# Two-layer kernel behind linear attention: where the second layer's weights and inputs are split into hi and lo, and in which order its first product runs

## The chip, the cores and the metric

The kernel runs on one core of a Trainium2 chip. The metric is device time in microseconds of one execution, as the median of the runs shown. TensorE (PE), VectorE (DVE), ScalarE (ACT), GpSimd (POOL) and SyncE (SP) run side by side; SP issues most transfers, POOL some.

## The reference

```python
q_s = softmax(q, axis=-1); k_s = softmax(k, axis=2)        # with 1e-9 in the divisor
kv  = einsum('bhsd,bhse->bhde', k_s, v)
x   = einsum('bhsd,bhde->bhse', q_s, kv)                   # 8 x 8 heads x 576 x 64
x   = x.transpose(0, 2, 1, 3).reshape(4608, 512)
x   = (relu(x @ w_in1) ** 2) @ w_out1                      # layer 1: 512 -> 2048 -> 512
h   = x @ w_in2
out = (h * (1 / (1 + exp(-h)))) @ w_out2                   # layer 2: 512 -> 2048 -> 512
```

All is float32. The kernel multiplies float32 in three passes of a narrower format: each operand is split into hi (the rounded value) and lo (the rest), and wh·xh + wh·xl + wl·xh is summed.

## The kernel before

**Tiling.** The 4608 tokens are nine blocks of 512 (NB = 9). The hidden width of 2048 is 16 slices of 128 (NF), or eight chunks of 256 (NG).

**First layer.** For each block, 16 steps ("slots") run: `layer_in(f)` is 12 matmuls of 512 columns for one slice, `hidden` makes Relu on ACT, the square (on DVE, but on ACT in the first and last block), and a copy to hi on ACT; `hidden_lo` subtracts on DVE; `layer_out` adds the slice into four PSUM banks two slots later. Beside it stand the next block's attention (`side`, by slot) and the preparation of the second layer's weights: `round_to_dram` loads one of 32 pieces of raw weights, rounds it (one ACT and three DVE operations for each half; phase 3's pieces also an ACT copy that permutes columns) and writes it to `wd` in DRAM from POOL. It is a generator: it goes on by two steps a slot. After a block's last slice `layer_out` copies the four banks into `x2_tile`, makes four sums and writes the seven slots for that block to `x2d` from SP.

**Second layer.** It multiplies by a seven-product scheme on halves of 256: `PRODUCTS` lists which slot of the input (A11, S3, S2, S1, A12, A22, S4) goes with which weight (B11, T3, T2, T1, B21, N4, B22). Blocks go in pairs (`supers`): four pairs, 512 columns wide, and the last block alone, 256 wide. Phase 2 computes h for all of them in the order 0, 1, 2, 4 (the narrow one), 3; phase 3 computes out in the order 0 to 4. A step is one product of one chunk: six matmuls. In phase 2 the chunk j is the outer loop and the product n the inner one; in phase 3 the product is outer and the chunk inner.

`seven(ph, x)` makes one chunk's weight set in SBUF: four loads of 128 KB from `wd` on SP, four subtracts on POOL, then for each of the seven a copy to hi on ACT and a subtract to lo on DVE. It runs in the last block (for phase 2) and in the last pair of phase 2 (for phase 3). `factor(u, n)` loads the two halves of one input slot from `x2d` and `a_split` splits them on ACT and DVE; a pair's factors stay for all eight chunks and are replaced, one by one, in the last chunk of the pair before. Phase 3's inputs come through `stream`: loaded 14 steps ahead (`a_load`), split 6 steps ahead (`a_split`).

`after` evicts a product: ACT copies it or makes Silu, DVE adds it to earlier ones in an output tile `st` (two such tiles; `g_tile` and `x2_tile` have the same two places before). After the seventh product POOL writes two slots to `g2d`, one sum is made on POOL and three on DVE, and POOL writes the rest.

**What orders the work.** 89 tiles of 256 KB ("rooms") are handed out and taken back in a queue by `room` and `back`; a load starts when the room's last reader is done. Eight PSUM banks go round in the same way. From the last block of the first layer on every engine keeps program order (`keep_in_program_order`); before that the framework orders the instructions of each engine by its own plan. All engine calls pass through `InOrder.call` (line 73), so the trace has L73 for all and is read by tile names: `al` and `ah` are lo and hi of an input, `wB`, `wT`, `wN` the weight sets, `a` to `e` PSUM banks of the products, `h` and `acc` those of the first layer.

## Time and profile before

| | us |
|---|---|
| runs (three) | 1642.99, 1646.23, 1646.77; median 1646.23 |
| the profiled execution | 1643.94 |
| its span | 1642.2 |
| PE busy | 1575.8 (96%) |
| DVE busy | 1121.7 (68%) |
| ACT busy | 738.1 (45%) |
| POOL busy | 288.0 (18%) |
| mean granted clock of PE | 0.989 |

The span goes from the first instruction's start to the last one's end. A busy share counts instructions that run; matmuls overlap one another, so PE's busy time is longer than what its columns need, and idle time on PE is what stands between them. A wait is put down to the engine and tile that ended it. A granted clock of 1.00 is 2.4 GHz, 0.5 is 1.2 GHz.

### The profile page before, as it was taken

What the parts mean: (1) busy time and instruction counts of PE and PEld (TensorE: products, weight loads), DVE (VectorE), ACT (ScalarE), POOL (GpSimd) and SP (SyncE); (2) the same over time, 40 slices, a digit from 0 to 9 for tenths busy, and PEclk for the clock granted to TensorE, in tenths of its full rate; (3) what the DMA queues carried; (4) which work ended last, traced back from release to release, by engine and by line L of the source; (5) the groups of instructions that cost most, each with busy time, mean ns of one, the idle gap of its engine ahead of it and who ended that gap; (6) DMA issues with size and microseconds to landing.
All of it is one profiled execution on the core that took longest, in us unless ns stands there. A gap on an engine that the chain in (4) does not pass through costs nothing. (4 is left out here: it accounts for less than half of the span.)

```text
span 1642.2 us, 23717 instructions
## 1 busy us (share of the span) xinstructions
PE 1575.8 (96%) x7672; PEld 1293.0 (79%) x7672; DVE 1121.7 (68%) x2284; ACT 738.1 (45%) x1562; POOL 288.0 (18%) x517
## 2 busy tenths in 40 slices
PE   5999999999999999999999999998998799999998
PEld 3767888877878888888888778787976688888888
DVE  8999676676757677672356776767778856656565
ACT  7875343333434344342365343333344644444433
POOL 2000101000101010000022534444756300000000
PEclk9999999999999999999999999999999899999999
DMA  9635343343524434230233565655667668676845
GB/s 261 194 111 158 113 149 113 101 145 92 158 85 132 129 109 143 86 122 0 76 111 105 196 243 205 244 194 216 234 216 278 236 194 246 195 243 179 260 127 166
DMA packets 225787, 269.49 MB, mean 164 GB/s; under 512 B 61568, under 2 KB 159616, under 8 KB 225664
## 3 DMA queue, kind: packets, MB, share of 16 engines
q1 hardware_dynamic: 202416, 193.01, 39.5%
q0 software_dynamic: 21888, 74.46, 12.1%
q8 instruction: 60, 0.98, 0.2%
q10 hardware_dynamic: 1360, 0.52, 0.1%
q14 instruction: 63, 0.52, 0.1%
HBM read 160.17 MB, written 107.74 MB: 163 GB/s over the span
## 5 line engine op out<-in xcount | busy, mean ns | idle before, releaser
L73 PE MATMUL h<-x,wh 128*128 128x512 f32 x1152 | 359.7, 392 | 5.2 <-ACT wh L73 3.3
L73 PE MATMUL acc<-st,wh 128*128 128x512 f32 x1152 | 361.2, 393 | 0.3 <-DVE st L73 0.3
L73 PEld LDWEIGHTS h<-x,wh 128*128 128x128 f32 x1152 | 215.4, 188 | 55.6 <-ACT wh L73 6.6
L73 ACT CAST ah<-al 128x512 fp32r<-128x512 f32 (+1 forms) x350 | 195.4, 578 | 140.5 <-PE d L73 39.6
L73 PEld LDWEIGHTS acc<-st,wh 128*128 128x128 f32 x1152 | 213.2, 188 | 45.7 <-DVE st L73 1.5
L73 DVE TENSOR_TENSOR al<-al,ah 128x512 fp32r<-128x512 f32 (+1 forms) x350 | 206.0, 644 | 50.2 <-ACT ah L73 47.1
L73 PE MATMUL h<-x,wl 128*128 128x512 f32 x576 | 225.3, 391 | 0.2 <-DVE wl L73 0.2
L73 PE MATMUL acc<-st,wl 128*128 128x512 f32 x576 | 224.4, 390 | 0.0
L73 PE MATMUL a<-ah,wB 128*128 128x512 f32 (+1 forms) x640 | 199.8, 375 | 8.6 <-DVE wB L73 6.8
L73 ACT ACTIVATE st<-st 128x512 f32<-128x512 f32 (+1 forms) x120 | 70.7, 589 | 230.7 <-DVE st L73 180.2
L73 ACT ACTIVATE g<-h 128x512 f32<-128x512 f32 x144 | 85.6, 594 | 172.5 <-PE h L73 172.1
L73 DVE TENSOR_TENSOR st<-g,st 128x512 fp32r<-128x512 f32 x144 | 100.0, 695 | 80.5 <-ACT st L73 72.9
L73 PEld LDWEIGHTS a<-ah,wB 128*128 128x128 f32 x640 | 119.9, 193 | 31.3 <-DVE wB L73 8.4
L73 DVE TENSOR_TENSOR st<-st 128x512 f32<-128x512 f32 (+1 forms) x156 | 131.5, 848 | 6.7 <-ACT ah L73 0.5
L73 DVE TENSOR_TENSOR g<-g 128x512 f32<-128x512 f32 x112 | 76.8, 685 | 85.8 <-ACT g L73 85.7
L73 POOL DMA_DIRECT2D g2d<-st x200 | 111.5, 562 | 116.9 <-ACT st L73 87.8
L73 PEld LDWEIGHTS h<-x,wl 128*128 128x128 f32 x576 | 108.3, 188 | 24.0 <-DVE wl L73 1.7
L73 PEld LDWEIGHTS acc<-st,wl 128*128 128x128 f32 x576 | 108.1, 188 | 23.2
L73 ACT CAST st<-g 128x512 fp32r<-128x512 f32 x144 | 89.4, 621 | 74.3 <-DVE g L73 73.2
L73 PE MATMUL a<-al,wB 128*128 128x512 f32 (+1 forms) x320 | 119.7, 374 | 0.2 <-DVE al L73 0.2
L73 PE MATMUL d<-ah,wB 128*128 128x512 f32 (+1 forms) x320 | 100.4, 377 | 10.8 <-DVE st L73 8.6
L73 PE MATMUL b<-ah,wT 128*128 128x512 f32 (+1 forms) x320 | 98.9, 372 | 3.4 <-ACT ah L73 3.4
(131 smaller groups left out, 2496.9 us busy)
## 6 DMA issues: line engine op xcount, KB each, us to landing
al<-g2d SPq DMA_DIRECT2D x224, 256.0 KB, 3.2
g2d<-st POOLq DMA_DIRECT2D x64, 512.0 KB, 3.0
g2d<-st POOLq DMA_DIRECT2D x112, 256.0 KB, 3.6
wraw<-in_moe_w_in_dram SPq DMA_DIRECT2D x64, 256.0 KB, 3.2
wraw<-in_moe_w_out_dram SPq DMA_DIRECT2D x64, 256.0 KB, 3.3
x2d<-st SPq DMA_DIRECT2D x18, 896.0 KB, 6.0
al<-x2d SPq DMA_DIRECT2D x56, 256.0 KB, 3.9
v<-in_v_dram SPq DMA_DIRECT2D x64, 128.0 KB, 2.8
```

What stands on the lines that cost most here:

```text
L73: got = fn(*a, **kw)
```

## The change

- `seven` is no longer run in the second layer. It runs in blocks 1 to 7 of the first layer, two or three sets a block (`SETS`): it loads the raw rows of a chunk, rounds them (phase 3's permutation is now part of the last DVE add, in two pieces), makes the four differences on DVE, splits all seven, and writes each product's hi and lo (256 KB) to `wd` from POOL. Its scratch is the seven rows of `x2_tile`. `round_to_dram` is gone.
- `w_load` loads one product's weights of one chunk, hi and lo, into a room: 56 loads for each phase, for phase 2 in the last block, for phase 3 in the last pair as rooms come free, product by product.
- `layer_out` hands the end of a block to a generator, `keep_outputs`: copies, sums, then for each of seven slots a copy to hi on ACT, a subtract in place on DVE, and two writes to `x2d` from POOL. It goes on during the next block's first slots; for the last block during phase 2's first steps.
- `factor` is four loads (hi and lo of both halves) and no split.
- Phase 2 takes the chunks in pairs: for each product first chunk j, then j + 1, with two sets of PSUM banks and both `st` tiles in use.
- All squares of the first layer are on ACT, all sums of `after` on DVE.

```diff
-    def round_to_dram(ph, f):
...
+    def seven(ph, x, places):
+        lo_, hi_ = slice(0, HB), slice(HB, TB)
+        r0, r1, u0, u1, t, *ws = places
+        raw = [raw_load(ph, x), raw_load(ph, NG + x, (r0, r1))]
         for _ in range(3):
             yield
+        for r, u in zip(raw, (u0, u1)):
+            yield from rounding(ph, r, u, t)
...
+        ws = (*ws, r0, r1)
+        ve.tensor_tensor(t3, b22, b12, op=ALU.subtract)
+        ve.tensor_tensor(b12, b12, b11, op=ALU.subtract)
         yield
+        ve.tensor_tensor(t2, b22, b12, op=ALU.subtract)
+        yield
+        all_ = dict(B21=b21, B11=b11, T3=t3, T2=t2, T1=b12, N4=b21, B22=b22)
+        for m, (name, v) in enumerate(all_.items()):
+            w = ws[m % 4]
+            hi, lo = w[:, lo_], w[:, hi_]
+            ac.copy(hi.bitcast(F32R), v)
+            ve.tensor_tensor(lo, v, hi, op=ALU.subtract)
+            if m == 0:
+                ve.tensor_tensor(b21, b21, t2, op=ALU.subtract)
+            gp.dma_start(out=wd[ph, x][:, names.index(name)], in_=w)
             yield
+    def w_load(ph, x, n):
+        w = W[ph, x, n] = room(F32R, "w")
+        sp.dma_start(out=f32(w), in_=wd[ph, x][:, n])
...
     def hidden(i, n, h):
-        if i in (0, NB - 1):
-            ac.activation(g, g, AF.Square)
-        else:
-            ve.tensor_tensor(g, g, g, op=ALU.mult)
+        ac.activation(g, g, AF.Square)
...
+    def keep_outputs(i):
...
+        yield
         sums(lambda s: t[:, :, s], ve)
+        yield
         u, b = divmod(i, 2)
-        for e in range(2):
-            sp.dma_start(out=x2d[u][e][:, :, b * HB:(b + 1) * HB], in_=t[:, e])
+        for s, _ in PRODUCTS:
+            r = room(F32R, "x2h")
+            hi = r.rearrange("p (e c) -> p e c", e=2)
+            ac.copy(hi, t[:, :, s])
+            ve.tensor_tensor(t[:, :, s], t[:, :, s], f32(hi), op=ALU.subtract)
+            for j, x in enumerate((f32(hi), t[:, :, s])):
+                gp.dma_start(out=x2d[u][:, :, s, j, b * HB:(b + 1) * HB], in_=x)
+            back(r)
+            yield
...
+            for js in ([range(j, j + 2) for j in range(0, NG, 2)] if ph == 2 else [range(NG)]):
+                for n in range(7):
+                    for j in js:
+                        steps.append((ph, u, n, j, u == us[-1]))
...
+        if ph == 2:
+            hi = room(F32R, "ah")
+            for j, t in enumerate((hi, lo)):
+                sp.dma_start(out=f32(t)[:, o], in_=x2d[u][:, c, slot, j])
...
-                sums(at_, ve, gp)
+                sums(at_, ve)
...
+    def load_todo(spare):
+        while todo and len(rooms) >= todo[0][0] + spare:
+            todo.pop(0)[1]()
...
+    SETS = [0, 2, 2, 2, 2, 2, 3, 3, 0]
+            s = SETS[i]
+            for m in range(s + 1):
+                if not doing and made < len(w2list) and s and 3 <= f < NF - 2 and made < sum(SETS[:i + 1]):
+                    doing.append(seven(*w2list[made], [x2_tile[:, x] for x in range(7)]))
+                    made += 1
+                go_on()
...
+            todo += [(1, lambda x=x, m=m: w_load(3, x, m)) for m in range(7) for x in range(NG)]
```

## Rows read from the trace of the kernel before

**Rows 1.** The page, part 1: busy us, share of span, instructions.

```profile
PE 1575.8 (96%) x7672; PEld 1293.0 (79%) x7672; DVE 1121.7 (68%) x2284; ACT 738.1 (45%) x1562; POOL 288.0 (18%) x517
```

**Rows 2.** Stretches: length, busy us of each engine, granted clock, DMA share, GB/s.

```profile
0.00:36.50 36.50, 19.80 (x122) 11.83 (x122) 28.72 (x101) 25.09 (x88) 6.69 (x23) 1.00 0.96 273
36.50:888.90 852.40, 842.93 (x4190) 687.86 (x4191) 581.22 (x1353) 389.72 (x848) 78.62 (x218) 1.00 0.38 115
888.90:1277.50 388.60, 362.75 (x1681) 298.22 (x1680) 284.85 (x439) 154.74 (x320) 191.20 (x263) 0.97 0.63 226
1277.50:1299.57 22.07, 15.26 (x50) 11.25 (x49) 19.14 (x27) 10.42 (x25) 11.52 (x14) 0.81 0.59 209
```

**Rows 3.** Timeline of PE: start us, us; first matmuls of phases 2 and 3.

```profile
888.93 0.39 PE L73 MATMUL a<-ah,wB 128*128 128x512 f32 x1
...
1277.53 0.63 PE L73 MATMUL a<-ah,wB 128*128 128x512 f32 x1
```

**Rows 4.** Chain that ended last, in order of time: start us, us, what.

```profile
1332.74 10.88 PE a L73 x48
...
1617.53 5.76 PE a L73 x48
```

**Rows 5.** Stretches, one for each pair of blocks of phase 2; columns as before.

```profile
888.90:969.00 80.10, 77.75 (x333) 62.98 (x332) 58.19 (x89) 31.42 (x66) 33.96 (x46) 0.98 0.57 208
969.00:1052.00 83.00, 79.85 (x337) 64.67 (x336) 58.71 (x79) 30.69 (x54) 35.39 (x48) 0.96 0.60 220
1052.00:1136.40 84.40, 80.73 (x343) 64.96 (x342) 59.99 (x81) 31.49 (x57) 35.98 (x49) 0.98 0.59 221
1136.40:1184.20 47.80, 43.39 (x337) 42.14 (x336) 34.36 (x75) 18.43 (x53) 31.89 (x47) 0.96 0.60 202
1184.20:1277.50 93.30, 81.04 (x338) 63.47 (x337) 73.60 (x117) 42.71 (x94) 53.99 (x73) 0.98 0.74 263
```

**Rows 6.** Waits of PE from 888.9 to 1299.6: us, times, longest.

```profile
PE d L73 <- DVE st L73: 8.6, 5, 4.7
PE a L73 <- DVE wB L73: 6.8, 2, 4.7
PE b L73 <- DVE al L73: 6.7, 4, 2.0
```

**Rows 7.** Stretches of 4 us at the change to the second pair of blocks.

```profile
968.00:972.00 4.00, 3.97 (x17) 2.78 (x15) 2.35 (x4) 3.05 (x6) 0.54 (x1) 1.00 1.03 399
972.00:976.00 4.00, 1.98 (x7) 1.05 (x6) 3.86 (x6) 2.56 (x6) 1.83 (x2) 1.00 1.02 400
976.00:980.00 4.00, 2.90 (x7) 2.32 (x8) 4.00 (x8) 2.73 (x6) 2.01 (x4) 0.53 0.77 291
```

**Rows 8.** Groups of instructions by form: count, busy us, mean ns, idle before.

```profile
L73 DVE TENSOR_TENSOR al<-al,ah 128x512 fp32r<-128x512 f32 x280 | 180.8, 701 | 38.9 <-ACT ah L73 36.6 <-DMA al<-x2d 1.3 <-DMA al<-g2d 0.7
L73 ACT CAST ah<-al 128x512 fp32r<-128x512 f32 x280 | 169.2, 621 | 121.8 <-PE d L73 33.9 <-PE a L73 22.8 <-PE e L73 20.6
L73 POOL DMA_DIRECT2D g2d<-st x200 | 111.5, 562 | 116.9 <-ACT st L73 87.8 <-ACT wB L73 18.6 <-ACT wT L73 6.8
L73 DVE TENSOR_TENSOR g<-g 128x512 f32<-128x512 f32 x112 | 76.8, 685 | 85.8 <-ACT g L73 85.7
L73 POOL TENSOR_TENSOR st<-st 128x512 f32<-128x512 f32 x32 | 56.6, 1768 | 80.1 <-DVE st L73 44.7 <-ACT st L73 35.5
L73 DVE TENSOR_TENSOR wB<-wB 128x256 fp32r<-128x256 f32 x48 | 22.7, 488 | 8.6 <-ACT wB L73 5.3 <-issue 3.2
L73 ACT ACTIVATE g<-g 128x512 f32<-128x512 f32 x32 | 20.2, 630 | 0.6
```

**Rows 9.** Timeline of DVE: four sums alone, three beside POOL's one.

```profile
889.92 2.75 DVE L73 TENSOR_TENSOR st<-st 128x512 f32<-128x512 f32 x4
...
987.42 3.10 DVE L73 TENSOR_TENSOR st<-st 128x512 f32<-128x512 f32 x3
```

**Rows 10.** DMA issues: KB each, median us from issue to landing.

```profile
wd<-wu POOLq DMA_DIRECT2D x16, 256.0 KB, 3.3
```

More of the change, by code (lines that the diff above doesn't have):

```diff
@@ L142 @@
     x2d = [
-        [dpool.tile([P, 7, len(bl) * HB], F32, name=f"x2d{u}_{e}") for e in range(2)]
-        for u, bl in enumerate(supers)
+        dpool.tile([P, 2, 7, 2, len(bl) * HB], F32, name=f"x2d{u}") for u, bl in enumerate(supers)
     ]
@@ L149 @@
     ]
-    wd = {(ph, f): dpool.tile([P, DM], F32, name=f"wd{ph}_{f}") for ph in (2, 3) for f in range(NF)}
+    wd = {(ph, x): dpool.tile([P, 7, TB], F32, name=f"wd{ph}_{x}") for ph in (2, 3) for x in range(NG)}
     A21, A11, A22, A12, S1, S2, S4 = range(7)
@@ L196, in rounding @@
             )
-            ve.tensor_tensor(o, o, lw, op=ALU.add)
-            back(t)
-            yield
-        if ph == 3:
-            v = room(F32, "wp")
-            ac.copy(
-                v.rearrange("p (e a i) -> p a e i", e=P // Q, a=P // Q),
-                u.rearrange("p (a e i) -> p a e i", e=P // Q, a=P // Q),
-            )
-            back(u)
-            u = v
-        to.append(u)
-    def rounded(ph, raw):
-        to = []
-        for _ in rounding(ph, raw, to):
-            pass
-        return to[0]
+            if ph == 3:
+                to = u.bitcast(I32).rearrange("p (e a i) -> p a e i", e=P // Q, a=P // Q)
+                o, lw = (x.rearrange("p (a e i) -> p a e i", a=2, i=Q) for x in (o, lw))
+                for a in range(2):
+                    ve.tensor_tensor(to[:, 2 * h + a], o[:, a], lw[:, a], op=ALU.add)
+            else:
+                ve.tensor_tensor(o, o, lw, op=ALU.add)
+            if id(t) in lent:
+                back(t)
+            yield
     wh1, wl1, raw1 = {}, {}, {}
@@ L223, in w1_round @@
     def w1_round(x):
-        raw1[x] = rounded(x[0], raw1[x])
+        u = room(F32, "wu")
+        for _ in rounding(x[0], raw1[x], u):
+            pass
+        raw1[x] = u
     def w1_split(x):
@@ L719, in a_load @@
         slot = PRODUCTS[n][0]
-        w = width(u)
-        src = (x2d if ph == 2 else g2d)[u][c]
-        sp.dma_start(out=f32(lo)[:, 0:w], in_=src[:, slot])
-        xs[ph, u, n, c] = [None, lo]
+        o = slice(0, width(u))
+        if ph == 2:
+            hi = room(F32R, "ah")
+            for j, t in enumerate((hi, lo)):
+                sp.dma_start(out=f32(t)[:, o], in_=x2d[u][:, c, slot, j])
+        else:
+            hi = None
+            sp.dma_start(out=f32(lo)[:, o], in_=g2d[u][c][:, slot])
+        xs[ph, u, n, c] = [hi, lo]
     def a_split(ph, u, n, c):
@@ L953 @@
             if n == (NB - 1) * NF:
-                assert nw == len(w2list) and not doing
+                assert made == len(w2list) and not doing
                 back(*kv_rooms[1:])
-                todo = [(9, lambda g=g: seven(2, g, gp)) for g in range(NG)]
-                todo[4:4] = [(4, lambda m=m: factor(LAST_LONG[0], m)) for m in range(7)]
+                todo += [(1, lambda x=x, m=m: w_load(2, x, m)) for x in range(NG) for m in range(7)]
+                todo[28:28] = [(4, lambda m=m: factor(LAST_LONG[0], m)) for m in range(7)]
             if n == NF:
@@ L976 @@
             hidden_lo(n)
-            if not ends:
-                for _ in range(2):
-                    go_on()
-                if i > 0 and nw < len(w2list) and not doing:
-                    doing.append(round_to_dram(*w2list[nw]))
-                    next(doing[-1])
-                    nw += 1
+            s = SETS[i]
[4 more added lines that the diff above has]
+                go_on()
+            if f == NF - 1:
+                assert not doing
+            if ends:
+                load_todo(3)
         else:
@@ L987 @@
                 back(wh1.pop((1, f)), wl1.pop((1, f)))
-                for _ in range(3):
-                    while todo and len(doing) < 3 and len(rooms) - owed[0] >= todo[0][0]:
-                        begin()
-                    go_on()
+                load_todo(3)
     back(*x_rooms, *g_rooms)
```

127 lines of the change are left out of this document (32 added, 95 removed).

## The prediction

> **What bounds the kernel now.** I read the page's busy shares first, then one table of stretches, then TensorE's waits, then what stands around those waits. TensorE (PE) is busy for 96% of the span [rows 1], so only time in which PE stands still or runs at half clock can be won. The table of stretches [rows 2] says where that is: the first layer, 852.4 us long, has 9.5 us of idle PE, and the second layer's first product (phase 2) has 25.9 us in 388.6 us. The first product of phase 3 takes 22.1 us and has 6.8 us idle. How long they could be comes from the chain that ended last: 48 matmuls of 512 columns take 10.88 us and 48 of 256 columns 5.76 us when nothing interrupts them [rows 4], that is 0.2267 and 0.120 us each. Phase 2 has 336 matmuls for each of the five pairs of blocks, four of them wide and one (the last block alone) narrow: 4 x 336 x 0.2267 + 336 x 0.120 = 304.6 + 40.3 = 345.0 us. Its first matmul starts at 888.93 and phase 3's at 1277.53 [rows 3]: 388.6 us, **43.6 us too many**. Phase 3's first product, 48 matmuls, should take 10.9 us and takes 22.0: **11.1 us too many**. Together 54.7 us; the change works nowhere else on the path, so this is nearly all that it can win.
>
> Pair by pair the excess is 3.9, 6.8, 8.2, 7.5 and 17.1 us, each length less 76.2, the short one less 40.3 [rows 5]. The waits name the causes [rows 6]: PE waits for DVE's evictions (8.6 us), for weight sets still being split (6.8) and for factors still being split (6.7). Some of the stops are followed by a granted clock near 0.5, the 1.2 GHz level: 0.53 just after a stretch in which PE was busy 1.98 of 4 us [rows 7]. The first pair's 0.98 over 80.1 us [rows 5] is one such dip and 1.6 us of lost clock; I count 1.7 us for a dip.
>
> **Part by part. Taken out of phase 2:** the 70 splits of factors, each a copy on ACT and a subtract on DVE (0.62 and 0.70 us wide [rows 8]); the splits of the weight sets on both; POOL's subtracts and its share of the sums. One of POOL's adds takes 1.77 us [rows 8], and while it runs DVE's three other sums take 3.1 us; four sums on DVE with POOL quiet take 2.75 us [rows 9]. So the move of the fourth sum onto DVE costs nothing: it even gives back 0.35 us a chunk. What was waited for in [rows 6] is then gone: weights and factors arrive by DMA ready to be multiplied. Next late in their place can only be the DMA itself, which I cost below.
>
> **The pairs of chunks.** A product of one chunk takes 1.36 us, of two 2.72, so a pair takes 19.04 us. DVE's work on it is 10 adds and 8 sums at about 0.69 us: 12.4 us, it fits. PSUM: at most six of eight banks are open at once. The two output tiles (st) are now wanted again sooner: the last product of a first chunk ends 17.7 us into its pair, then add, Silu, sums, and its last write lands about 3.3 us after POOL issues it, as the weights' writes do [rows 10], some 25.3 us into the pair; the next pair writes that tile from about 26.7 us on. DVE waits 0 to 1 us there, and PE would feel it only when DVE is some 5 us late. I take nothing.
>
> **Moved into the first layer.** By the rows' durations [rows 8], DVE loses 112 squares (76.7 us) and gains 16 x 11 half-width operations at 0.49 (86 us) and 56 wide splits at 0.70 (39 us): from 581 to some 630 of 852 us [rows 2]. ACT gains 112 squares at 0.63 (71 us), 112 half-width copies (35 to 70 us, as half or all of a wide one) and 56 wide ones (35 us): from 390 to about 550. POOL issues 80 weight writes and 112 factor writes more at 0.56: about 108 us, beside 79 now. No engine is near its limit, and PE runs two layer-in products ahead of each layer-out. What may hurt is order: seven() works in x2_tile, which keep_outputs() uses too. The load of its second raw rows waits on SP until POOL's last write from that place has landed (3.3 us after its issue [rows 10], plus copy, subtract and issue: some 6 us), and queued behind it are the loads of q, k and v and the round trip of the transposed queries, for which ACT and then PE wait. A slot is about 6 us, so most of it is covered. Bounds: below, a gain of 1 us (SP loses the writes of x2); above, 16 sets x 1 us. I take **3 us**.
>
> **Start of phase 2.** Block 8's seven products are split beside the first products and written by 14 POOL issues, at 0.56 us each. The second output tile is x2_tile's place; those writes, the first some 2 us into phase 2, have landed by about 13 us. PE first feels that DVE waits for it at the seventh product, 16.3 us in, less 1.4 us of DVE work. Covered by some 2 us; I take **1 us** instead of 3.9.
>
> **The transfers.** This is the open term. Factors now take 28 loads of 256 KB between pairs of blocks (7.34 MB) where 14 did, and each weight set of 1.83 MB is read where 0.5 MB was. The room of factor m comes free in the last pair of chunks, and it is wanted one pair later: from 2.7 us into that pair to 35.4 us, 32.7 us for 7.34 MB plus some 5.9 MB of g2d writes (1.83 MB a chunk): 13.2 MB. What can the DMA engines move? In the fullest stretches 399 and 400 GB/s at a share of 1.02 to 1.03 [rows 7]; with small packets 273 at 0.96, or 284 when full [rows 2]. The transfers here are those of rows 7, so I take 390. Then 13.2 MB take 33.9 us: **1.1 us** late at each of two wide changes, and 0.5 us at the narrow one. From the narrow to the last wide pair the window is 25 us for 10.3 MB, 26.4 us: **1.4 us**. In the last pair of blocks the 56 sets for phase 3 are read as rooms come free, ahead of phase 3's first inputs on the same queue. From the first factor load to the eighth input: 7.3 MB of factors, 14.9 MB of sets and inputs, 17.7 MB of writes, 40 MB or 102.5 us, against 91.9 us of matmuls: 10.6 late, less the 1.4 already counted and about 1.5 of writes that can follow: 7.7 us, with a clock dip of 1.7: **9.4 us**.
>
> The Trainium skill (DMA: Bandwidth & Descriptors, section Bandwidth) speaks against that: it has transfers between HBM and SBUF bound at about 358 GB/s for a core. By that figure the residue would be 38.5 us and the time 1628, rival B. The stretches at 399 and 400 GB/s disagree with it; the page itself gives more to a core that streams alone.
>
> **Sum.** Residue: 3 + 1 + 1.1 + 1.1 + 0.5 + 1.4 + 9.4 = 17.5 us. The profiled execution took 1643.94 us, 1.74 us around its span of 1642.2 and 2.3 below the median of the three runs. 1643.94 - 54.7 + 17.5 = 1606.7, said as **1607 us**. About 0.3% (5 us) is what can be told from no change here.
>
> **Rivals.**
> *A. Transfers hide wholly* (phase 3's inputs in time): the residue is 3 to 9 us, 1592 to 1598. For it: the full stretches touch 400. Against: 40 MB in 92 us would want 435.
> *B. The DMA ceiling is lower under reads and writes mixed over 90 us.* A quarter of the way from 390 to 284, at some 360 GB/s, the same sums give 1 + 11.4 (both wide changes, with dips) + 1 + 5.3 + 15.8 + 3 = 37.5: 1627. At 340, about half the way, the residue is 49: 1638. For it: no pair of blocks averages above 263 GB/s [rows 5]. Against: there nothing asked for more.
> *C. Slower, by the same mechanism in the last wide pair and at the start of phase 3:* below about 332 GB/s the residue passes 54.7 us and the kernel loses; at the 284 of the first 36 us it would be 90 us, 1679. Against it: those are small packets, phase 2 moves 2 KB runs.
> *D. The first layer stalls:* SP's wait for x2_tile outlasts its cover. It decides when each of the 16 sets costs PE over 2.3 us, as 16 x 2.3 eats the 37 us; half of that gives 1625. For it: SP carries all loads of attention. Against: PE hardly waits there now.
> *E. POOL's issues slow down beside DVE.* If each took the 1.77 us of POOL's add, the 14 at the start of phase 2 would end 17 us later and PE would stop about 15.5 us, with a dip: 1624. The Trainium skill (SBUF — State Buffer, "SBUF: two separate sides") warns of it: a POOL-issued DMA waits for its descriptors while DVE holds the shared ports. The 200 issues at 562 ns beside a busy DVE do not show it [rows 8].
> *F. The change does not do what it says:* sets arrive too late for the first pair, so the first pair of blocks keeps its 3.9 us and a dip; 1611. The rooms freed in the last block allow all loads by then.
>
> **How the numbers follow.** Forecast (1600 to 1616) 0.50, A 0.15, B 0.18, C 0.03, D 0.09, E 0.02, F 0.03. To leave out no more than 2 in 10 the range goes from 1594 (most of A) to 1632 (B down to about 350 GB/s, the milder half of D). Slower by over 0.3%: C and the worst of D, 0.05; within 0.3%: the edge of B and D, 0.05; faster 0.90.
>
> **What would show it.** Right: phase 2 takes about 350 us from its first matmul to phase 3's, PE's waits for al and wB are gone, DVE has no al subtract there; phase 3's first product stays visibly above 10.9 us with ACT or PE waiting for a DMA from g2d; stretches near 390 GB/s in the last wide pair. Wrong: if that first product takes 11 us (A), if long waits stand at each change of blocks (B), or if 36.5 to 889 has grown by over 10 us (D). I would be wrong altogether if the evictions of two chunks at once held PE in every pair.

## The result, and the profile after

The changed kernel took **1666.55 us** (median of 4 runs, 1664.14 to 1670.69) against 1644.61 for the kernel before on the same chip: ratio **1.0146**, 95% interval 1.0128 to 1.0164 (the two medians alone give 1.0133, inside it). It is slower by about 22 us where 1607 was forecast. The profiled execution took 1670.69 us, 26.8 more than the one of before.

First the table of stretches: length, busy us of each engine with its instructions, granted clock, DMA share, GB/s. The bounds are the first matmuls of phase 2 (917.65) and phase 3 (1306.85) and the end of phase 3's first product.

```profile
36.50:917.65 881.15, 858.62 (x4205) 697.29 (x4203) 584.67 (x1462) 495.81 (x1071) 175.90 (x382) 0.99 0.52 166
917.65:1306.85 389.20, 359.04 (x1681) 299.65 (x1680) 214.97 (x363) 105.53 (x208) 115.03 (x205) 0.96 0.77 284
1306.85:1323.00 16.15, 13.05 (x50) 9.63 (x49) 13.10 (x22) 8.20 (x15) 4.82 (x9) 0.89 1.05 397
```

Against [rows 2, 3]: the first layer's end has moved from 888.93 to 917.65, **28.7 us lost**; phase 2 lasts 389.2 instead of 388.6, **nothing won**; from phase 3's first matmul to the last one it is 354.2 instead of 357.0, 2.8 won. The sum is 26.5 of the 26.8. So there are two questions: what costs the first layer 28.7 us, and where phase 2's expected gain went. In neither is it idle time alone: in the first layer PE stands idle for 22.5 us instead of 9.5, and is busy for 858.6 instead of 842.9 us, as its clock falls behind the stops; in phase 2, 30.2 of the 44.2 us above the 345.0 worked out from [rows 4] are idle. The waits name a place for each (us, times, longest):

```profile
DVE st L74 <- DMA g2d<-st: 111.2, 32, 6.8
PE d L74 <- DVE st L74: 24.2, 12, 3.6
PE xps L74 <- DVE kvs L74: 13.5, 5, 4.6
```

In phase 2, PE's waits for al and wB in [rows 6] are gone, as forecast (3.0 us for al stay in phase 3's first product). In their place DVE waits 32 times for the store of an output tile (st) to land, which it never did before, and PE waits for DVE behind that. In the first layer PE now stops once in each of five blocks for the state of the attention (kvs).

**Phase 2, pair of blocks by pair of blocks** (columns as above; the bounds are the first matmul of each):

```profile
917.65:1002.28 84.63, 78.66 (x338) 63.97 (x337) 50.13 (x78) 27.00 (x48) 26.28 (x45) 0.98 0.71 258
1002.28:1084.08 81.80, 78.37 (x337) 64.06 (x336) 46.56 (x73) 21.80 (x40) 21.40 (x40) 0.98 0.72 271
1084.08:1161.57 77.49, 76.77 (x337) 62.91 (x336) 44.97 (x71) 21.04 (x39) 21.43 (x40) 1.00 0.68 252
1161.57:1219.17 57.60, 44.38 (x338) 43.08 (x336) 30.02 (x74) 14.03 (x42) 23.90 (x40) 0.89 0.70 250
1219.17:1306.85 87.68, 80.86 (x337) 65.63 (x337) 43.29 (x71) 21.66 (x40) 22.02 (x40) 0.95 0.99 373
```

Less 76.2 and, for the narrow one, 40.3, the excess is 8.4, 5.6, 1.3, **17.3** and 11.5 us. The largest single piece lies in the narrow pair of blocks, which was 7.5 before [rows 5].

**Phase 2, the last pair of chunks of the first pair of blocks.** Here the factors of the second pair of blocks are loaded. The timelines of DVE, POOL and PE show the chain (start us, us, instruction, in brackets the idle time before it and its releaser):

```profile
989.19 0.69 DVE L74 TENSOR_TENSOR st<-c,u 128x512 f32<-128x512 f32 x1 [2.57 <-DMA g2d<-st]
989.80 0.68 DVE L74 TENSOR_TENSOR u<-b,u 128x512 f32<-128x512 f32 x1
996.49 0.69 DVE L74 TENSOR_TENSOR st<-c,u 128x512 f32<-128x512 f32 x1 [6.01 <-DMA g2d<-st]
```

```profile
983.94 2.14 POOL L74 DMA_DIRECT2D g2d<-st  x4 [0.66 <-DVE st L74]
```

```profile
997.83 0.50 PE L74 MATMUL d<-ah,w 128*128 128x512 f32 x1 [2.49 <-DVE st L74]
```

DVE stands 2.57 us for the first chunk's tile and 6.01 us for the second's, both because the stores of the pair of chunks before have not landed: the last of them were issued by 986.1 and DVE goes on at 996.5. Its later adds come late and PE stops. Meanwhile the transfer engines are full, which the stretches of 4 us show:

```profile
984.00:988.00 4.00, 4.00 (x20) 3.30 (x19) 1.13 (x2) 0.00 (x0) 2.08 (x4) 1.00 1.02 396
988.00:992.00 4.00, 4.00 (x19) 3.31 (x18) 1.29 (x2) 0.00 (x0) 0.00 (x0) 1.00 1.03 390
992.00:996.00 4.00, 3.34 (x15) 2.44 (x13) 0.00 (x0) 0.00 (x0) 0.00 (x0) 1.00 1.04 397
996.00:1000.00 4.00, 2.17 (x7) 1.75 (x8) 3.08 (x5) 2.14 (x5) 0.13 (x1) 0.83 1.05 400
```

The stores share those engines with the loads of factors. The list of DMA issues (KB each, median us to landing) has them at 5.2 and 6.2 us; before they landed in 3.0 and 3.6, and I had assumed 3.3 [rows 10].

```profile
g2d<-st POOLq DMA_DIRECT2D x64, 512.0 KB, 5.2
g2d<-st POOLq DMA_DIRECT2D x112, 256.0 KB, 6.2
```

**The first layer, the block at 286 us.** `kv_norm` makes kvs from kvps, the product of keys and values, and begins with a reciprocal of one column (rc). Timelines of PE and of DVE:

```profile
275.02 0.29 PE L74 MATMUL kvps<-v 128*64 128x65 f32 x4
...
285.94 0.66 PE L74 MATMUL xps<-qh,st 128*128 128x384 f32 x1 [4.57 <-DVE kvs L74]
```

```profile
281.24 0.71 DVE L74 STREAM_TRANSPOSE q<-xr 128x512 f32<-128x512 f32 x1
282.56 0.29 DVE L74 TENSOR_SCALAR st<-st 128x256 int32<-128x256 int32 x1 [0.61 <-DMA st<-in_moe_w_in_dram]
282.89 0.16 DVE L74 TENSOR_SCALAR rc<-kvps 128x1 f32<-128x1 f32 x1
...
285.50 0.29 DVE L74 SCALAR_TENSOR_TENSOR kvs<-kvps,rc,st 64x64 fp32r<-64x64 f32 x1
```

PE has the kvps matmuls done at 275.3. rc comes on DVE only at 282.89: ahead of it in DVE's list stand steps of the next attention, the rest of a weight set, and then the rounding of the block's *second* set, whose raw words land at 282.5. DVE itself is idle for only 1.2 us of that time, so it is the length of the list more than one landing that holds rc back. Such a stop stands at 285.94, 386.5, 484.77, 581.5 and 681.25. The clock falls behind four of the five: the stretches of 40 us from 280, 380, 576 and 676 us have 0.91, 0.96, 0.96 and 0.96, where the kernel before had 1.00 over the whole first layer [rows 2].

### The profile page after: what moved, and what is told of

It reads as the page before. It is cut to its first block, busy times and chain, and to the rows that moved or that the text cites. A ratio compares the mean times of both kernels' runs of the same rounds, so it can differ in the third digit from the quotient of the medians.

```text
span 1668.9 us, 24370 instructions
## 1 busy us (share of the span) xinstructions
PE 1586.4 (95%) x7672; PEld 1302.3 (78%) x7672; DVE 1047.0 (63%) x2301; ACT 787.8 (47%) x1651; POOL 302.3 (18%) x619
## 4 chain that ended last, share of the span: by engine, by line
PE 29%; issue 12%; DMA 10%; DVE 5%; POOL 3%; ACT 1%; SPq 0%; DVEq 0%; POOLq 0%; ACTq 0%
PE d L74 10%; PE a L74 8%; DMA g2d<-st 7%; DVE st L74 4%; PE b L74 4%; PE e L74 4%; PE c L74 4%; POOL x2d L74 1%; DMA st<-in_moe_w_out_dram 1%; POOL wd L74 1%; ACT st L74 1%; POOL g2d L74 1%; DMA x2d<-st 1%; DMA wd<-st 0%; SPq L74 0%
## 5 line engine op out<-in xcount | busy, mean ns | idle before, releaser
L74 ACT ACTIVATE st<-st 128x512 f32<-128x512 f32 (+2 forms) x152 | 80.9, 556 | 307.3 <-DVE st L74 280.6
L74 ACT CAST ah<-al 128x512 fp32r<-128x512 f32 (+1 forms) x280 | 158.3, 579 | 135.9 <-PE d L74 40.3
L74 PE MATMUL d<-ah,w 128*128 128x512 f32 (+1 forms) x640 | 197.2, 381 | 24.2 <-DVE st L74 24.2
L74 DVE TENSOR_TENSOR st<-st 128x256 f32<-128x256 f32 (+1 forms) x372 | 191.3, 539 | 26.3 <-ACT st L74 18.5
L74 PE MATMUL a<-ah,w 128*128 128x512 f32 (+1 forms) x640 | 190.6, 371 | 0.1
L74 DVE TENSOR_TENSOR al<-al,ah 128x512 fp32r<-128x512 f32 (+1 forms) x280 | 159.8, 630 | 46.3 <-ACT ah L74 45.9
L74 PEld LDWEIGHTS d<-ah,w 128*128 128x128 f32 x640 | 121.5, 196 | 49.8 <-DVE st L74 28.8
L74 PEld LDWEIGHTS a<-ah,w 128*128 128x128 f32 x640 | 118.1, 191 | 20.9 <-ACT ah L74 0.5
L74 PEld LDWEIGHTS h<-x,wl 128*128 128x128 f32 x576 | 109.0, 189 | 24.4 <-DVE wl L74 1.7
L74 PE MATMUL a<-al,w 128*128 128x512 f32 (+1 forms) x320 | 118.7, 371 | 3.0 <-DVE al L74 3.0
L74 PE MATMUL d<-al,w 128*128 128x512 f32 (+1 forms) x320 | 121.4, 379 | 0.0
L74 PE MATMUL e<-ah,w 128*128 128x512 f32 (+1 forms) x320 | 95.1, 369 | 6.0 <-DVE st L74 4.5
```

What stands on the lines that cost most here:

```text
L74: got = fn(*a, **kw)
```

## The experiments

All compare with the kernel before on the same chip. "Layer 1" is the first matmul of phase 2, "phase 2" the time from there to phase 3's first matmul, in the profiled execution. Both columns are of one execution each. The changed kernel, e1, e3 and e4 have the same source in the first layer and lie between 911.29 and 920.18; kernels with the same source in phase 2 lie within 4 us. Smaller differences say nothing.

| kernel | median us | ratio, 95% interval | layer 1 | phase 2 |
|---|---|---|---|---|
| changed | 1666.55 | 1.0146, 1.0128 to 1.0164 | 917.65 | 389.2 |
| e1_unpaired | 1659.23 | 1.0106, 1.0074 to 1.0138 | 913.55 | 389.3 |
| e2_places | 1672.72 | 1.0183, 1.0154 to 1.0212 | 919.88 | 389.5 |
| e3_once | 1649.59 | 1.0033, 1.0018 to 1.0048 | 920.18 | 369.2 |
| e4_early | 1667.51 | 1.0137, 1.0117 to 1.0158 | 911.29 | 389.1 |
| e5_lead | 1669.27 | 1.0162, 1.0135 to 1.0188 | 917.58 | 388.5 |
| e6_nolo | 1675.83 | 1.0208, 1.0186 to 1.0230 | 917.07 | 389.4 |
| e7_whole | 1618.97 | 0.9856, 0.9835 to 0.9877 | 888.59 | 374.4 |
| e8_both | 1619.07 | 0.9857, 0.9834 to 0.9880 | 886.01 | 374.8 |
| e9_quick | 1678.79 | 1.0216, 1.0192 to 1.0240 | 922.98 | 389.0 |
| e10_shift | 1620.79 | 0.9855, 0.9833 to 0.9878 | 890.72 | 374.9 |
| e11_pairs | 1645.33 | 1.0014, 0.9997 to 1.0032 | 883.96 | 394.3 |
| e12_own | 1672.82 | 1.0173, 1.0156 to 1.0190 | 920.57 | 392.5 |
| e13_soon | 1612.86 | 0.9807, 0.9790 to 0.9823 | 887.60 | 369.2 |
| e14_work | 1622.29 | 0.9863, 0.9848 to 0.9878 | 891.39 | 376.9 |
| e15_stores | 1682.56 | 1.0222, 1.0195 to 1.0250 | 956.32 | 374.9 |
| e16_sp | 1644.82 | 1.0004, 0.9992 to 1.0016 | 893.32 | 391.1 |
| e17_pin | 1652.15 | 1.0061, 1.0039 to 1.0083 | 894.89 | 388.7 |
| e18_pinsoon | 1617.81 | 0.9841, 0.9825 to 0.9857 | 889.48 | 372.3 |

### Phase 2: pairs, loads and stores

**e1_unpaired**: chunk by chunk.

```diff
-            for js in ([range(j, j + 2) for j in range(0, NG, 2)] if ph == 2 else [range(NG)]):
+            for js in ([range(j, j + 1) for j in range(NG)] if ph == 2 else [range(NG)]):
```

> Phase 2 takes one chunk at a time again; all else as in the changed kernel. Theory (two output tiles, wanted again after 8 us in pairs and after some 13 us one by one, are held by g2d writes that share the DMA engines with loads): DVE's waits for g2d writes, 111 us in the changed kernel, fall to under 20 us, and PE's waits for st (24 us) to under 6. In their place PE waits for factors, since 7.3 MB at 400 GB/s take 18 us and a factor is wanted 9.5 us after its room comes free: 6 to 10 us at each of the three wide changes, so that phase 2 stays at 370 to 390 us. Rival (factors are early in any order, and only the output tiles cost): phase 2 falls to 350 to 358 us and the time to 1630 to 1640.

Phase 2 stays at 389.3, but for another reason. DVE's wait for stores is gone; PE now waits for the factors themselves, 17 us in all, on rows such as these (its waits from 913.55 us on):

```profile
PE d L74 <- DMA al<-x2d: 4.1, 8, 1.4
PE b L74 <- DMA al<-x2d: 3.0, 4, 1.5
PE d L74 <- DMA ah<-x2d: 2.9, 5, 1.2
```

So the pairs did what they say, they gave the loads time, and the stores paid for it. Phase 3's first product takes 10.88 us here, with the same loads, and 16.14 in pairs.

**e3_once**: the factors of the first pair of blocks are kept for all pairs, so the later pairs' own inputs are left out.

```diff
-                hi, lo = xs[ph, u, n, c]
+                hi, lo = xs[ph, LAST_LONG[0], n, c]
```

> The first pair's factors stay for all pairs of blocks: no factor is loaded after the first pair, so that phase 2 of the later pairs multiplies the first pair's inputs. All sums, evictions and writes stay. Theory (the writes are late because the factor loads take half of the DMA engines' time): the stops at the changes of blocks, 5.3, 5.7, some 8 and some 8 us, go, and those of the last wide pair, 10.8 us, with phase 3's weight loads, stay: phase 2 falls from 389 to 360 to 366 us, the time to 1638 to 1645. Rival (two tiles are too few for pairs even without loads): stops of at least 3 us stay at the changes, 1655 or more.

Without the loads phase 2 falls by 20 us to 369.2, 3 us above the range that I gave. DVE's wait for stores falls only from 111.2 to 82.5 us, and the stores still land in 4.6 and 5.0 us: two chunks' stores go out together in any case. What this costs depends on the width. The third pair of blocks, then the narrow one:

```profile
1076.77:1152.93 76.16, 76.16 (x337) 63.10 (x336) 46.89 (x73) 22.54 (x41) 21.42 (x40) 1.00 0.52 194
1152.93:1206.43 53.50, 44.84 (x337) 44.10 (x336) 29.50 (x74) 13.49 (x41) 23.89 (x40) 0.91 0.50 174
```

In the second and third pair of blocks DVE waits 8 times, up to 4.7 us, and PE does not stop once: 76.16 us is what the matmuls need. The narrow pair takes 13.2 us more than its 40.3 with the transfer engines half idle. A pair of narrow chunks lasts 14 x 6 x 0.120 = 10.1 us instead of 19.04, so the tiles are wanted back sooner, and the first such pair wants those of a wide one. It takes 16.7 us (1152.93 to 1169.65):

```profile
1166.12 0.42 DVE L74 TENSOR_TENSOR st<-c,u 128x256 f32<-128x256 f32 x1 [4.91 <-DMA g2d<-st]
```

```profile
1166.93 0.58 PE L74 MATMUL d<-ah,w 128*128 128x256 f32 x1 [5.01 <-DVE st L74]
```

**e4_early**: three of the four sums and five of the seven stored slots ahead of the last add.

```diff
+            if ph == 2:
+                gp.dma_start(out=g2d[u][x][:, A11:A22 + 1], in_=t[:, A11:A22 + 1, 0:w])
+                sums(at_, ve, 0)
+                ...
             ve.tensor_tensor(at_(c12), p, U2, op=ALU.add)
```

> The three sums that don't need the seventh product, and their writes, stand ahead of its eviction instead of behind it. Theory (late writes hold the output tiles): each pair's writes begin 2 to 4 us earlier, DVE's waits for g2d writes fall by a third or more, and phase 2 is 8 to 20 us shorter: 1646 to 1658. Rival (the DMA engines are full anyway, so the last write lands at the same time): under 5 us, 1661 to 1668.

Phase 2 389.1. DVE's wait for stores falls from 111.2 to 96.9 us, but PE's wait for st behind it stays at 24.4: the earlier issue wins nothing. That full transfer engines are the reason was my rival; this run doesn't show it by itself.

**e7_whole**: the factors stored whole by SP and split in phase 2, as before; chunk by chunk; the weight sets stay in the first layer.

```diff
-            for j, x in enumerate((f32(hi), t[:, :, s])):
-                gp.dma_start(out=x2d[u][:, :, s, j, b * HB:(b + 1) * HB], in_=x)
+        for e in range(2):
+            sp.dma_start(out=x2d[u][e][:, :, b * HB:(b + 1) * HB], in_=t[:, e])
...
+        for _ in range(8):
+            yield
+        for c in range(2):
+            a_split(2, u, n, c)
```

> The changed kernel with the inputs' factors as in the kernel before: stored whole by SP at each block's end (14 loads per change of pair and a split in phase 2 on ScalarE and VectorE instead of 28 loads and no split), phase 2 chunk by chunk; the weight sets stay made in the first layer. If the factors' bytes are what fills the DMA engines at each change, phase 2 falls from 389 (e1_unpaired) to 370 to 380 and phase 3 starts without a stop; the first layer loses VectorE and ScalarE some 39 and 35 us and 126 stores: phase 2 at 900 to 912 if the rest of that loss lies with the weight sets. Time 1625 to 1648. Rival: the splits are late as in the kernel before (9.0 us on al and 6.0 on ah there), phase 2 stays at 385 to 390 and the time is 1645 to 1658.

**e11_pairs**: e7_whole in pairs of chunks (the diff of e1_unpaired, the other way).

> The changed kernel with the inputs' factors whole as in e7_whole, but phase 2's first product in pairs of chunks as in the changed kernel: the pairing by itself. With half of the factors' loads the stores of the second layer's hidden values should land in 3.0 to 4 us again, but each pair asks for its two scratch tiles again 8 us after the last use: the waits of VectorE on stores are 40 to 90 us instead of 111.2, and phase 2 lasts 372 to 383 against e7_whole's 374.4. If pairing costs nothing once the loads are halved: 366 to 372. If the second tile's early use is a cost even then: 383 to 392.

e7_whole is the first kernel to beat the one before, by 1.4%, more than I had expected: phase 2 lasts 374.4 us, and each of phase 3's first three products takes its 10.88. With half of the bytes at a change of blocks the loads are in time (PE waits for the splits, 8.0 us on al, not for a DMA) and the stores land as before. These are its phase 2 and its stores:

```profile
888.59:1262.99 374.40, 356.66 (x1682) 296.85 (x1680) 258.01 (x427) 141.10 (x269) 107.79 (x196) 0.98 0.70 256
```

```profile
g2d<-st POOLq DMA_DIRECT2D x64, 512.0 KB, 3.0
g2d<-st POOLq DMA_DIRECT2D x112, 256.0 KB, 3.5
```

And in e11_pairs, with the same loads and the same splits:

```profile
883.96:1278.28 394.32, 362.68 (x1681) 302.24 (x1680) 244.59 (x419) 130.87 (x264) 105.10 (x191) 0.96 0.65 240
```

```profile
g2d<-st POOLq DMA_DIRECT2D x64, 512.0 KB, 4.7
g2d<-st POOLq DMA_DIRECT2D x112, 256.0 KB, 5.3
```

```profile
PE d L74 <- DVE st L74: 25.9, 13, 4.3
```

**Pairing alone costs 19.9 us** of phase 2 here; 394.3 is above the highest that I had expected (392). Phase 3's first two products take 8.7 us more as well. Two chunks finish together, their 3.7 MB of stores go out together and land later, and each of the two tiles is wanted again sooner. With whole factors it has nothing to give for that. Most of it lies in the narrow pair of blocks, first in e7_whole, then in e11_pairs:

```profile
1133.99:1181.65 47.66, 44.08 (x338) 43.20 (x337) 34.45 (x84) 19.00 (x53) 23.61 (x39) 0.93 0.64 213
```

```profile
1129.56:1192.64 63.08, 47.91 (x337) 46.16 (x336) 36.25 (x86) 19.47 (x55) 23.86 (x41) 0.85 0.58 205
```

That is 15.4 of the 19.9. The two costs do not add up: chunk by chunk with whole factors phase 2 takes 374.4 us (e7), with split factors 389.3 (e1), in pairs with whole factors 394.3 (e11), in pairs with split factors 389.2 (the changed kernel).

**e13_soon**: e7_whole with the splits issued earlier.

```diff
-        for _ in range(8):
+        for _ in range(5):
```

> e7_whole with the splits in phase 2 issued five generator turns after their loads instead of eight (two turns per product). TensorE waits 7.9 us on al and 3.5 on ah in e7_whole, while ScalarE waits for none of those loads: if the splits stand too late in the order, phase 2 falls from 374.4 to 366 to 372; if the loads are then waited for, it stays within 3 us. Time 1609 to 1622.

Phase 2 falls to 369.2 and the kernel takes **1612.86 us, the fastest of all**, 1.9% below the kernel before. The splits of e7_whole stood too late in the order: PE's waits for al fall from 8.0 to 2.6 us.

### The first layer

**e2_places**: a weight set's second raw rows go out of their places first, so that the next set's load need not wait for POOL's last store (rival D as I had written it).

```diff
-        ws = (*ws, r0, r1)
+        ws = (r0, r1, *ws, t, *ws)
...
-            w = ws[m % 4]
+            w = ws[m]
```

> In seven() the places of the second raw rows are used for the first two products only, and a tile that is done after the fourth takes their turn, so that the next set's raw load finds its places written out long ago. Theory (SP's raw load waits for POOL's write; ACT and DVE wait for the load ahead of the attention's work; PE waits for kvs): PE's wait for kvs, 13.5 us, falls under 6, the low clock in the first layer goes with it, and the first layer is 12 to 20 us shorter: 1647 to 1655. Rival (the longer first layer comes from more work on ACT, or from the squares): no change beyond 4 us, 1663 to 1670.

Layer 1 at 919.88, though SP's wait for a set's own stores between 130 and 800 us falls from 56.6 to 26.1 us: not this wait.

**e5_lead**: raw words asked for during the set before.

```diff
             gp.dma_start(out=wd[ph, x][:, names.index(name)], in_=w)
+            if m == 4 and made < last[0]:
+                ahead[w2list[made]] = raws(*w2list[made])
```

> The changed kernel with the raw words of the next weight set asked for while the present set is still being stored (after its fifth product; and at the block's third slot for the first set of a block), instead of one slot ahead of their rounding; places 0 and 1 are written out first so that they are free by then. Theory L (late loads): the first layer lost 28.7 us because ScalarE and VectorE stand in order at the rounding of raw words that have not landed (at 282.6 us in the changed kernel both wait for such a load, with kv_norm's work behind), and TensorE's five stops (13.5 us on kvs) and the low-clock stretches behind them are what follows. It expects the kvs wait at 5 us or less, phase 2's first matmul at 892 to 902 instead of 917.65, and a time of 1641 to 1656. Theory B (bunching: the sheer work on VectorE and ScalarE within a slot): kvs wait still over 10, phase 2 at 912 to 920, time 1660 to 1672.

Layer 1 at 917.58. The earlier loads hold rooms for longer, and SP then stands for rooms instead (its waits on kvps between 130 and 800 us are 155.1 us, 79.7 in the changed kernel); PE waits 9.0 us on kvs and 11.3 on qh. Loads alone are not it.

**e6_nolo**: no lo halves of the weight sets are made; what is stored in their place is left over.

```diff
-            ve.tensor_tensor(lo, v, hi, op=ALU.subtract)
```

> The changed kernel without the 112 subtractions on VectorE that make the lo halves of the weight sets in the first layer (the lo halves stored are whatever stood there, so layer 2's values are not computed; every load, copy and store stays). About 47 us of VectorE's work leaves the blocks 1 to 7. Theory B (sheer work on VectorE): the kvs wait falls to 5 us or less and phase 2 starts at 890 to 903. Theory L (late loads): the wait stays at 9 us or more and phase 2 starts at 908 to 918, time 1657 to 1668.

917.07, with 47 us less work on DVE: not the amount of work. e7_whole above gave the first layer back whole (888.59), by leaving out the split of the *inputs* and their 14 stores a block.

**e9_quick** and **e10_shift**: the splits of the inputs two at a time, so that the weight sets start a slot earlier; and e7_whole with the sets a slot later.

```diff
+            if k % 2:
+                yield
...
-                if not doing and made < len(w2list) and s and 3 <= f < NF - 2 and made < sum(SETS[:i + 1]):
+                if not doing and made < len(w2list) and s and (4 if s == 2 else 3) <= f < NF - 2 and made < sum(SETS[:i + 1]):
```

> The changed kernel with the splits of the second layer's inputs done two at a time at the start of each block instead of one, so that they end a slot earlier and the first weight set of a block starts at the block's slot 3 instead of slot 4; all its work, loads and stores stay. Theory S (slots): the splits themselves are not what the first layer pays for; they push the weight sets one slot back, and the second set's rounding then falls on the slot where VectorE has the third pair of heads' kv_norm to do (the one stop per block, at 285.94, 386.5, 484.77, 581.5 and 681.25 us in the changed kernel). It expects phase 2's first matmul at 887 to 897 and the kvs wait at 4 us or less, time 1635 to 1650. Theory W (work): ScalarE's 35 us and VectorE's 39 us of splits, with their stores, are the cost wherever they stand: phase 2 at 908 to 920, time 1658 to 1672.

> e7_whole with the weight sets of the blocks that have two of them started at the block's slot 4 instead of slot 3; nothing else. Theory S: the stop per block is back (kvs wait 8 us or more) and phase 2 starts at 905 to 918 instead of 888.59, time 1635 to 1650. Theory W: phase 2 stays at 886 to 893 and the time within 0.3 per cent of e7_whole's 1619.

922.98 and 890.72: the slot in which the sets start is not it.

**e12_own** and **e14_work**: the splits' hi halves in four rooms of their own; and the splits' work alone, in e7_whole, without a store.

```diff
-            r = room(F32R, "x2h")
+            r = own[k % 4] if own else room(F32R, "x2h")
```

```diff
+            ac.copy(hi, t[:, :, s])
+            ve.tensor_tensor(hi, t[:, :, s], f32(hi), op=ALU.subtract)
```

> The changed kernel with the hi halves of the inputs' splits in four rooms that are held until the splits of a block are done, instead of a new room for each that goes back at once and is handed to the next loads. Work, stores and their queue stay. Theory R (rooms): SP's queue stands 9 to 16 us per block at a load into a room whose store has not landed (82.1 us in all between 130 and 800 us), every load behind it comes late, and TensorE's stops follow. It expects that wait under 20 us, kvs wait 4 us or less, phase 2's first matmul at 888 to 900, time 1636 to 1653. Theory P (POOL and the stores' bytes) and theory W (work): phase 2 at 910 to 920, time 1658 to 1672.

> e7_whole (factors whole) with the splits of the inputs done in the first layer all the same, 7 copies on ScalarE and 7 subtractions on VectorE per block, whose result nobody reads and nothing stores. Theory W: phase 2 at 905 to 918 as in the changed kernel and time 1637 to 1650. Theories R and P: phase 2 at 886 to 896 and a time within 0.5 per cent of e7_whole's 1619.

In e12_own SP's wait for the stores of the hi halves falls from 82.1 to 22.5 us and waits on kvps (139.9 us) stand in its place; layer 1 is at 920.57. In e14_work the same work without the stores costs 2.8 us, less than kernels of one source differ. That leaves the stores.

**e15_stores** and **e16_sp**: 14 stores per block through POOL added to e7_whole; and the changed kernel's 14 stores moved to SP's queue.

```diff
+            for j in range(2):
+                gp.dma_start(out=more[u][:, :, s, j, b * HB:(b + 1) * HB], in_=t[:, :, s])
```

```diff
-                gp.dma_start(out=x2d[u][:, :, s, j, b * HB:(b + 1) * HB], in_=x)
+                sp.dma_start(out=x2d[u][:, :, s, j, b * HB:(b + 1) * HB], in_=x)
```

> e7_whole (factors whole, stored by SP) with the changed kernel's 14 stores per block through POOL's queue added, of the same sizes, to a place that nobody reads; no splitting. Theory P (the stores themselves: POOL's time to issue them, their bytes, and the weight sets' places, which are the same tile and come free only when they have landed): phase 2's first matmul at 900 to 916 instead of 888.59, kvs wait 5 us or more, time 1633 to 1648. If only stores that wait for ScalarE's and VectorE's splits cost (late stores, theory D: the first set's raw words go into the tile that they leave): phase 2 at 887 to 895, time within 0.5 per cent of 1619.

> The changed kernel with the 14 stores per block of the split inputs issued on SP's queue instead of POOL's. Theory P by POOL's issue time (some 0.55 us for each, 126 of them): phase 2 starts at 890 to 902 instead of 917.65, time 1640 to 1655. If their bytes or their late landing are the cost, or SP's loads standing behind them: phase 2 at 912 to 930, time 1660 to 1685.

e15_stores loses 67.7 us in the first layer against e7_whole, far over the 28 I had as an upper bound, so it does more than put the changed kernel's stores back, and that rest is not explained. e16_sp, with all work and all bytes of the changed kernel, gets **24.3 us back**; PE waits 1.5 us on kvs. The first layer's stretch, then DVE in the block that answers to the one at 286 us above (kvps done at 268.8 here):

```profile
36.50:893.32 856.82, 845.39 (x4194) 689.07 (x4192) 586.43 (x1461) 494.35 (x1069) 96.85 (x270) 1.00 0.54 171
```

```profile
270.76 0.16 DVE L74 TENSOR_SCALAR rc<-kvps 128x1 f32<-128x1 f32 x1
...
273.55 0.29 DVE L74 SCALAR_TENSOR_TENSOR kvs<-kvps,rc,st 64x64 fp32r<-64x64 f32 x1
...
274.48 0.29 DVE L74 TENSOR_SCALAR st<-wraw 128x256 int32<-128x256 int32 x1
```

Here rc follows kvps by 2 us, and the second set's rounding stands *behind* kvs. The order has changed, though the source of both is the same for these operations. Outside the last block the order of instructions on an engine isn't the written one: the program's builder lays them by its own plan. As written, a set goes on by three steps a slot. In VectorE's list of the changed kernel, 26 of the 46 operations of a block's two sets stand ahead of the first kvs of that block's second kv_norm, the whole first set (23) and 3 operations of the second; in e16_sp 23, in e14_work 24.

**e17_pin**: the changed kernel, stores on POOL, with the roundings of the sets held to the written order on ScalarE and VectorE; 11 of the 46 then stand ahead.

```diff
+            was, pinned[0] = pinned[0], pinned[0] or ph >= 2
             ac.activation(lw, lw.bitcast(U32), AF.Copy, scale=2.0 ** -29)
...
+            pinned[0] = was
```

> The changed kernel with the roundings of the weight sets held to the written order on ScalarE and VectorE (they may not be laid ahead of anything written before them); stores, work and queues stay. In the changed kernel VectorE's list has 26 of the 46 operations of a block's two sets ahead of that block's second kv_norm, here 11. Theory O (order): kv_norm stands behind set work laid too early, whose raw words have not landed; with the order held, the kvs wait falls to 4 us or less and phase 2's first matmul comes at 888 to 900 instead of 917.65, time 1636 to 1653. Theory P (POOL's queue itself, whatever the order): phase 2 at 908 to 922, time 1658 to 1675.

**22.8 of the 28.7 us come back**, with every store still on POOL's queue. Stretch and wait:

```profile
36.50:894.89 858.39, 845.53 (x4190) 688.37 (x4190) 585.22 (x1458) 489.16 (x1065) 177.74 (x382) 1.00 0.53 170
```

```profile
PE xps L74 <- DVE kvs L74: 4.5, 5, 1.4
```

So it takes two things. The order alone does no harm: e7_whole has 31 operations ahead of that kv_norm and loses nothing. There the sets are early: the first set's first store goes out 8.3 us after the block's first kvps, in the changed kernel 20.2 us after it. First the changed kernel, then e7_whole:

```profile
250.83 0.69 PE L74 MATMUL kvps<-v,k 128*64 128x65 f32 x16
...
271.01 1.22 POOL L74 DMA_DIRECT2D wd<-st  x2 [8.94 <-DVE st L74]
```

```profile
244.96 0.69 PE L74 MATMUL kvps<-v,k 128*64 128x65 f32 x16
...
253.28 0.56 POOL L74 DMA_DIRECT2D wd<-st  x1 [21.48 <-DVE st L74]
```

The lateness alone does little: in e16_sp that store comes 19.4 us after it (263.78 after 244.34) and in e17_pin 27.4 us (272.47 after 245.08), but nothing of the second set stands ahead. In e15_stores both are there, 30 operations ahead and 19.0 us (274.09 after 255.12), and its longest stop for kvs is 7.3 us. Late sets *and* kv_norm queued behind the second of them make the stop. That the order does harm is shown by e17_pin, which changes nothing else; that the lateness is the other half rests on comparing these kernels.

Two more: e8_both, e7_whole with the earlier raw loads of e5_lead, took 1619.07 us, as e7_whole did; and e18_pinsoon, e13_soon with the hold of e17_pin, took 1617.81 where I had expected 1608 to 1615, so the hold has nothing to give where the sets are in time.

## Why the prediction was wrong, point by point

**The first layer, "I take 3 us": 28.7.** This step failed most. The place was named ("what may hurt is order", rival D), and I said that it would show in a first layer longer by over 10 us. But I costed one wait, SP's for a weight set's own place, at up to 16 sets x 1 us, and took the written order of the slots for the order on the engines. What happened is DVE's list: kv_norm behind set work laid too early, which is 22.8 of the 28.7 us. e2_places shows that SP's wait was not it, e16_sp and e17_pin show what was. "No engine is near its limit" was right (DVE 585 and ACT 496 of 881 us) and proved nothing, as e6_nolo says.

**POOL's 112 input stores at 0.56 us each: 0.75 and 0.80** (busy time by count; the single records, which overlap, are 0.76 and 0.94 long). The price came from stores to another layout [rows 8]. The sum held even so, 97 us more on POOL in the first layer against 108 forecast. But "beside 79 now" hid that the 14 of a block go out in one row, ahead of what the tile they leave is wanted for.

**The pairs, "I take nothing": 17.3 us in the narrow pair of blocks alone.** The step failed where it was not taken: the turnaround of the output tiles was worked out for a wide pair of 19.04 us and for the first chunk's tile. For wide pairs without loads it holds (76.16 us in e3_once, and the threshold of "some 5 us" with it: DVE's waits of up to 4.7 us stop nothing there). The narrow pair, with 10.1 us for a pair of chunks, loses 13.2 us in e3_once with no factor loaded, 17.3 in the changed kernel. With loads the wide ones lose too: the landing of 3.3 us came from stores of the first layer, where the DMA share is 0.38 [rows 2, 10], and I costed the stores' bytes in the term of the transfers and left them out of this one. In the rows above, the first tile comes free 29.4 us into the pair that began at 959.82, where 25.3 was forecast, and the second chunk's, which I had not worked out, at 36.7; its wait of 6.01 us stopped PE by 2.49. What I said would refute me ("the evictions of two chunks at once held PE in every pair") is near to what happened.

**Start of phase 2, "I take 1 us": 4.1.** The first pair of chunks takes 23.13 us (917.65 to 940.78) instead of 19.04; in e11_pairs, without the seven splits and their stores, it takes 19.04. I had the stores landed 13 us into phase 2. ACT waits 4.63 us there for rooms that the first stores still hold, and DVE gets the tile 18.9 us into it.

**The transfers: nearly right in rate, wrong in who waits.** 390 GB/s was assumed; the stretches at the change of blocks have 396, 390, 397 and 400, the whole last wide pair 373 at a share of 0.99. That lies between my 390 and rival B's 360: 40 MB at 373 take 107 us instead of 102.5, so B can be a small part of the loss and C none. The Trainium skill (DMA: Bandwidth & Descriptors, section Bandwidth) says that for transfers between HBM and SBUF the HBM side binds, at about 358 GB/s for a core, and gives more to a core whose neighbour is idle; this trace has 390 to 400 for 16 us, so the lower figure was not the bound here. But the transfers delay one another where the engines are full. I let the loads be late by the overhang alone, 1.1 us a change, and the stores by nothing. In fact the loads were in time and the stores late; in e1_unpaired, with half the time for the loads, it is the other way round.

**Phase 3's start, 9.4 us:** phase 3's first two products take 16.14 and 13.88 us instead of 10.88, 8.3 us too many, behind a last wide pair that is itself 11.5 us late. That 8.3 is near 9.4 is luck: I had worked it out from bytes alone, and e1_unpaired, with the same loads, starts phase 3 with 10.88. The kernels of the table in pairs start it with 16.14 us or more, those chunk by chunk with 10.9. How the pairs delay it is not shown.

**Right:** PE's waits for al and wB are gone from phase 2; the sums on DVE alone are no problem; rivals E and F did not come. POOL's issues were slower than assumed for the inputs, but g2d's still took 0.557 us and wd's 0.544 beside a busy DVE.

Of the net loss, then: +28.7 in the first layer, +0.6 in phase 2, where 25.9 us of idle PE became 30 us of another kind, -2.8 behind it. What stays open: 6 us of the first layer that e17_pin leaves, which is within what kernels of one source differ by; and by what share POOL's slower issue, its queue and the later landing each make the sets late.

## What to carry to other kernels

Splitting an operand once and storing both halves doubles the bytes of every later load: it paid where the transfer engines had room (the weight sets here: e13_soon, with whole factors, gains 1.9%, though squares and sums moved along with them) and lost where they were already full at that moment (the factors, 14.9 us of phase 2 from e7_whole to e1_unpaired). Before taking a buffer's turnaround as free, put in the landing time of a store under the traffic that the change itself adds, and work it out for the narrowest block as well. And where a builder orders the instructions, read the order from its list: work that fits by its sum can still be laid ahead of the one operation that the critical engine waits for.

## What the runs showed of the hardware

The time that POOL needs to issue stores of the same size differs by group. The stores of these three have 256 KB each (line, engine, operation, count, busy us, mean ns, idle before):

```profile
L74 POOL DMA_DIRECT2D wd<-st x112 | 60.7, 544 | 168.1 <-DVE st L74 153.0 <-issue 5.0 <-DVE xr L74 3.3
L74 POOL DMA_DIRECT2D x2d<-st x63 | 50.3, 938 | 4.9 <-DVE st L74 4.2
L74 POOL DMA_DIRECT2D x2d<-x2h x63 | 47.2, 757 | 248.6 <-ACT x2h L74 240.4 <-issue 7.5
```

wd's stores write 128 pieces of 2 KB, x2d's 256 pieces of 1 KB. The mean is that of single records, which overlap when stores follow one another closely; by busy time and count a store holds POOL for 0.54, 0.80 and 0.75 us, and 0.72 us in e15_stores, again with 256 pieces. That the number of pieces is the reason is not shown by a run of its own.

A store's landing grows with the traffic around it. In e7_whole 512 KB and 256 KB to g2d take 3.0 and 3.5 us in the first pair of blocks (DMA share 0.61), 6.0 and 6.8 in the last (1.02). Stores that go out together wait for one another too: in e11_pairs they take 4.3 and 4.8 us in the third pair of blocks at a share of only 0.55.
